# Mixing matrices loaded as f32 on SyncE's queue and cast by ScalarE, with operand tiles by role and chunk stages placed by product slots

## The chip, the cores and the metric

The kernel runs on one core of one Trainium2 chip. The metric is the device time of that core in microseconds (us), the median of several executions. Each execution is sorted as fast or slow; the ratios below use fast ones alone, the medians all. On the profile's pages the engines are PE (TensorE matmuls), PEld (TensorE's weight loads), DVE (VectorE), ACT (ScalarE), POOL (GpSimd) and SP (SyncE). "SPq" and "POOLq" are instructions that an engine only issues, DMAs above all. "L336" is line 336 of that kernel.

## The reference, cut to what matters

```python
# x: 8 x 4224 x 192;  w_tok_r, w_tok_i: 4224 x 4224, all f32
x  = softmax_conv(x, weight)             # 7 taps, 8 groups of channels
theta = x @ w_theta
zr, zi = x * cos(theta), x * sin(theta)
y  = einsum('ts,bsd->btd', w_tok_r, zr) + einsum('ts,bsd->btd', w_tok_i, zi)
u  = x + y
return u + maximum(u @ w_ch, 0)
```

Nearly all the work is in the two 4224 x 4224 mixing matrices. They are read from HBM as f32 and multiplied as bf16.

## The kernel before

The 4224 tokens are 33 chunks of 128. The kernel makes 61 *visits*. A visit takes up to 11 chunks of `zr` and `zi` and (mostly) a pair of 128-row tiles of the output, and forms seven products for each half of a group of columns (a scheme in Strassen's manner, with operands `A11, A21, A22, A12` and their sums `S1` to `S4`). So a visit has 14 *product slots*. With 11 chunks a slot is 11 matmuls of 384 columns, planned at 1.79 us. For such a visit four tiles of weights are loaded, 4 DMAs each, transposed in 32 x 32 blocks by VectorE and summed by VectorE.

Some visits also prepare a chunk for later visits: convolution, two DMA transposes, the `theta` matmuls, clamping, sine and cosine. I call them **chunk visits**. These are visits 15 to 26 and 32 to 43; visits 15 and 32 prepare for the single-tile visits 16 and 33, visits 26 and 43 only finish the last chunk of their group, and the 18 between (17 to 25 and 34 to 42) are the *ordinary* ones. Visits 10 to 14 and 27 to 31 prepare nothing. Visits 0 to 9 are the **start** (1 to 10 chunks each) and 44 to 60 are the **tail**, where results are also finished and stored.

The parts that the change touches:

```python
    wpool = ctx.enter_context(tc.tile_pool(name="wpool", bufs=7))
    spool = ctx.enter_context(tc.tile_pool(name="spool", bufs=4))
    # ... cut
    class Weights:
        # ... cut
        def load(self):
            i = self.loads.pop(0)
            w = moe_w_tok_r if i[2] == "1" else moe_w_tok_i
            t = 2 * self.u + (i[1] == "2")
            st = spool.tile([P, NQ, SLOTS * Q], BF16, name="st", tag="st")
            for a in range(NQ):
                t0 = tokens(self.lo, a)
                nc.gpsimd.dma_start(             # casts f32 to bf16 on the way
                    out=st[a * Q : (a + 1) * Q, :, 0 : self.n * Q],
                    in_=w[t * P : (t + 1) * P, t0 : t0 + self.n * Q].rearrange(
                        "(bt i) s -> i bt s", bt=NQ
                    ),
                )
            self.st[i] = st
    # ... cut: step() transposes st into w by VectorE, or forms a sum S
    def chunk_events(c, t0, n):                  # times in us around t0
        for at, fn in (
            (-15.0, lambda: c + 2 < NCH and load_chunk(c + 2)),
            (-18.0, lambda: (chunks[c].conv(0), chunks[c].conv(1))),
            # ... cut
            (-14.0, lambda: chunks[c].transpose(0)),
            (-13.5, lambda: (chunks[c].transpose(1), chunks[c].keep())),
            (-5.0, lambda: chunks[c].theta(0)),
            (-2.5, lambda: chunks[c].theta(1)),
            (0.0, lambda: chunks[c].wave(0, 0)),
            # ... cut
    for v in range(len(visits)):                 # steps of visit v+1, loads of v+2
        # ... cut
        for frac, fn in (
            (0.4, lambda v=v: (start_weights(v + 2), step(v + 1), loads(v + 2, 1))),
            (2.4, lambda v=v: (step(v + 1), loads(v + 2, 1))),
            (2.9, lambda v=v: (step(v + 1), loads(v + 2, 1))),
            (4.4, lambda v=v: step(v + 1)),
            # ... cut
```

## Time and profile before

| | before |
|---|---|
| median (fastest to slowest) | 1540.75 us, 3 runs (1538.92 to 1586.56) |
| profiled run | 1555.2 us |
| start, up to visit 10 | 208.2 us |
| ten visits without a chunk | 250.2 us, 25.0 each |
| chunk visits | 660.1 us; the ordinary ones 29.0 on average |
| tail | 436.6 us |

A visit is timed from its first product matmul to that of the next, in the trace. These lines are from the page of the kernel before: the span, PE's busy time, then 40 equal slices of the span (the digit is the busy share in tenths; PEclk is the granted clock), and the two DMA queues that carry most of the bytes: queue, packets, MB, share of the 16 engines' time. q0 is GpSimd's queue.

```profile
span 1555.2 us, 25507 instructions
PE 1425.6 (92%) x9390; PEld 869.5 (56%) x9390; DVE 1078.8 (69%) x1818; ACT 336.5 (22%) x582; POOL 743.7 (48%) x1242
PE   5799999999999999999999999989999887878497
DMA  8999966559999999987889999999999999999995
q0 software_dynamic: 178496, 97.84, 49.4%
q1 hardware_dynamic: 94960, 180.56, 38.2%
```

PE is nearly always busy except at the two ends. The table of windows: the first row covers visits 11 to 14, without a chunk; the second covers visits 18 to 25, eight ordinary chunk visits.

```profile
core 0: us, PE busy (x) PEld busy (x) DVE busy (x) ACT busy (x) POOL busy (x), PEclk, DMA share, GB/s
233.30:333.40 100.10, 100.10 (x618) 60.27 (x617) 47.67 (x64) 19.52 (x40) 34.48 (x65) 1.00 0.63 122
403.10:634.70 231.60, 222.74 (x1493) 134.61 (x1490) 173.43 (x289) 47.57 (x81) 87.55 (x160) 0.99 1.10 207
```

Without a chunk PE never stops and DMA stands at a share of 0.63 and 122 GB/s. (The share is summed packet time over the time of 16 engines, and it can pass 1.) In chunk visits DMA is at 1.10 and 207 GB/s, and PE has 231.60 - 222.74 = 8.9 us of holes in eight visits. From the list of waits (engine, line, what it waited for, us in total, times, longest):

```profile
POOL st L327 <- DVE w L347: 429.5, 92, 11.3
PE v L301 <- DMA uT<-xz: 21.0, 15, 4.4
PE y L413 <- DVE d L431: 17.4, 3, 7.1
```

The first of these is harmless: GpSimd waits because its loads are *early* and all four buffers are full. The second is the wait that the new slot placement is aimed at: `theta` waits for the chunk's DMA transpose.

### The profile page before, as it was taken

What the parts mean: (1) busy time and instruction counts of PE and PEld (TensorE: products, weight loads), DVE (VectorE), ACT (ScalarE), POOL (GpSimd) and SP (SyncE); (2) the same over time, 40 slices, a digit from 0 to 9 for tenths busy, and PEclk for the clock granted to TensorE, in tenths of its full rate; (3) what the DMA queues carried; (4) which work ended last, traced back from release to release, by engine and by line L of the source; (5) the groups of instructions that cost most, each with busy time, mean ns of one, the idle gap of its engine ahead of it and who ended that gap; (6) DMA issues with size and microseconds to landing.
All of it is one profiled execution on the core that took longest, in us unless ns stands there. A gap on an engine that the chain in (4) does not pass through costs nothing.

```text
span 1555.2 us, 25507 instructions
## 1 busy us (share of the span) xinstructions
PE 1425.6 (92%) x9390; PEld 869.5 (56%) x9390; DVE 1078.8 (69%) x1818; ACT 336.5 (22%) x582; POOL 743.7 (48%) x1242
## 2 busy tenths in 40 slices
PE   5799999999999999999999999989999887878497
PEld 3455666656556556566665556655665554545354
DVE  6887854437777777776648877867886676667664
ACT  4654322122221221200002212212111111112111
POOL 9775433324334334332324343433577576666451
PEclk8999999999999999999999999999999998989699
DMA  8999966559999999987889999999999999999995
GB/s 103 232 213 194 181 122 126 121 115 207 207 213 203 210 205 205 223 197 177 182 178 203 223 215 205 208 178 208 242 191 218 231 223 201 244 210 224 188 200 133
DMA packets 361580, 301.65 MB, mean 194 GB/s; under 512 B 181008, under 2 KB 307984, under 8 KB 361456
## 3 DMA queue, kind: packets, MB, share of 16 engines
q0 software_dynamic: 178496, 97.84, 49.4%
q1 hardware_dynamic: 94960, 180.56, 38.2%
q10 hardware_dynamic: 88000, 21.64, 11.3%
q8 instruction: 73, 1.20, 0.3%
q14 instruction: 51, 0.42, 0.1%
HBM read 250.21 MB, written 106.56 MB: 229 GB/s over the span
## 4 chain that ended last, share of the span: by engine, by line
PE 61%; DMA 23%; DVE 5%; POOL 4%; issue 3%; ACT 3%; ACTq 1%; SPq 0%; DVEq 0%; POOLq 0%
PE y L413 25%; PE x L413 17%; PE s L413 14%; DMA uT<-xz 10%; PE v L301 3%; DMA ubT<-ubT 3%; DMA uT<-ub 2%; POOL st L327 2%; DMA xr<-xs 2%; DMA st<-in_moe_w_tok_i_dram 2%; PE pc L200 2%; DVE w L347 1%; DMA st<-in_moe_w_tok_r_dram 1%; ACTq L285 1%; DVE w L362 1%
## 5 line engine op out<-in xcount | busy, mean ns | idle before, releaser
L413 PEld LDWEIGHTS <-w 128*128 128x128 bf16 x6600 | 641.7, 98 | 449.2 <-issue 42.0
L327 POOL DMA_DIRECT2D st<-in_moe_w_tok_r_dram x476 | 258.9, 559 | 316.5 <-DVE w L347 194.2
L327 POOL DMA_DIRECT2D st<-in_moe_w_tok_i_dram x476 | 258.4, 558 | 314.2 <-DVE w L347 235.4
L347 DVE STREAM_TRANSPOSE w<-st 128x640 bf16<-128x640 bf16 (+4 forms) x324 | 258.2, 832 | 58.3 <-PE x L413 48.8
L431 DVE TENSOR_TENSOR d<-y,d 128x384 f32<-128x384 f32 x250 | 137.2, 553 | 179.3 <-PE y L413 165.5
L413 PE MATMUL y<-zr,w 128*128 128x384 bf16 x1056 | 191.2, 331 | 22.3 <-DVE d L431 17.4
L413 PE MATMUL x<-zr,w 128*128 128x384 bf16 x1122 | 203.0, 331 | 0.0
L413 PE MATMUL y<-zt,w 128*128 128x384 bf16 x1122 | 199.4, 328 | 3.8 <-ACT y L455 3.8
L413 PE MATMUL x<-zi,w 128*128 128x384 bf16 x1122 | 199.0, 327 | 0.0
L413 PE MATMUL y<-zt,wl 128*128 128x384 bf16 x1056 | 186.2, 330 | 0.0
L413 PE MATMUL s<-zt,w 128*128 128x384 bf16 x1056 | 184.7, 326 | 0.8 <-DVE late L431 0.7
L413 PE MATMUL s<-zi,w 128*128 128x384 bf16 x1056 | 184.7, 328 | 0.0
L362 DVE TENSOR_TENSOR w<-w 128x1408 bf16<-128x1408 bf16 (+10 forms) x174 | 146.8, 843 | 1.7 <-PE s L413 1.4
L413 PEld LDWEIGHTS <-wl 128*128 128x128 bf16 x1056 | 104.1, 99 | 67.7 <-issue 3.3
L243 ACT ACTIVATE zr<-ang,half_pi 128x768 bf16<-128x768 f32 x66 | 59.5, 929 | 318.4 <-PE y L413 238.9
L231 DVE TENSOR_SCALAR ang<-v 128x384 f32<-128x384 f32 x132 | 66.8, 545 | 55.3 <-PE v L301 55.0
L455 ACT ACTIVATE y<-x 128x384 f32<-128x384 f32 x116 | 55.3, 478 | 221.3 <-PE x L413 209.3
L431 DVE TENSOR_TENSOR d<-s,d 128x384 f32<-128x384 f32 x174 | 91.1, 536 | 11.4 <-PE s L413 9.3
L397 POOL TENSOR_TENSOR d<-d,xr 128x768 f32<-128x768 f32 x38 | 62.7, 1654 | 74.1 <-DMA xr<-xs 34.0
L301 PEld LDWEIGHTS <-uT 128*128 128x128 bf16 x704 | 60.9, 100 | 64.0 <-DMA uT<-xz 27.9
L188 POOL DMA_DIRECT2D xw<-in_x_dram x132 | 76.8, 599 | 38.5 <-PE pc L200 34.8
L347 DVE STREAM_TRANSPOSE wl<-st 128x640 bf16<-128x640 bf16 (+5 forms) x104 | 81.2, 814 | 11.7 <-DMA st<-in_moe_w_tok_i_dram 11.7
(72 smaller groups left out, 949.4 us busy)
## 6 DMA issues: line engine op xcount, KB each, us to landing
part<-d SPq DMA_DIRECT2D x172, 384.0 KB, 4.5
d<-part SPq DMA_DIRECT2D x144, 384.0 KB, 4.7
st<-in_moe_w_tok_r_dram POOLq DMA_DIRECT2D x316, 88.0 KB, 5.7
st<-in_moe_w_tok_i_dram POOLq DMA_DIRECT2D x316, 88.0 KB, 4.6
out_dram<-d SPq DMA_DIRECT2D x38, 384.0 KB, 5.8
xs<-xz SPq DMA_DIRECT2D x132, 96.0 KB, 5.3
xr<-xs POOLq DMA_DIRECT2D x66, 192.0 KB, 4.6
xw<-in_x_dram POOLq DMA_DIRECT2D x129, 96.0 KB, 7.9
```

The source lines that it names most:

```text
L188: nc.gpsimd.dma_start(out=self.xw[lo : lo + n, h, :, :], in_=x[:, t0 : t0 + n, :].rearrange("b s d -> s b d"),)
L200: pe(nc.tensor.matmul(pc[half * 2 * Q : (half + 1) * 2 * Q, hh * B * G : (hh + 1) * B * G], lhsT=bands[:, h, :, :].rearrange("p a m -> p ( ...
L231: dve(nc.vector.tensor_scalar(out=af[:, k * 2 * D : (k + 1) * 2 * D], in0=channel_mix(self.xT[g], k, wth), scalar1=-CLAMP, scalar2=CLAMP, ...
L243: act(nc.scalar.activation(out=z[:, g * HN : (g + 1) * HN], in_=self.ang[g], func=AT.Sin, **({"bias": half_pi[:], "scale": 1.0} if i == 0 ...
L301: pe(nc.tensor.matmul(v[:, b * D : (b + 1) * D], lhsT=tT[:, 3 * k + b + i, :], rhs=w[:, 2 * b + i, :], start=(i == 0), stop=(i == 1),), D)
L327: nc.gpsimd.dma_start(out=st[a * Q : (a + 1) * Q, :, 0 : self.n * Q], in_=w[t * P : (t + 1) * P, t0 : t0 + self.n * Q].rearrange("(bt i) s ...
L347: dve(nc.vector.transpose(w[:, c:ce, :, :], st[:, :, c * Q : ce * Q].rearrange("p bt (c j) -> p c bt j", j=Q),))
L362: dve(nc.vector.tensor_tensor(out=flat(o), in0=flat(self.w[p]), in1=flat(self.w[q]), op=op))
L397: nc.gpsimd.tensor_tensor(out=d, in0=d, in1=xr, op=ALU.add)
L413: pe(nc.tensor.matmul(y[:, 0:PC], lhsT=self.w.block(a, c), rhs=zs[c].operand(b, g), start=(start and c == self.lo), stop=(c == self.hi - 1 ...
L431: dve(nc.vector.tensor_tensor(out=o, in0=y[:, 0:PC], in1=o, op=ALU.add))
L455: act(nc.scalar.activation(out=y[g][:, 0:PC], in_=x[g][:, 0:PC], func=AT.Copy))
```

## The change

Its intent is to free GpSimd from writing descriptors for 952 casting DMAs, to place each step of the preparation at a product slot so that it keeps its place however long the visit is, and to keep one operand tile per role. The weights now go as f32 on SyncE's queue into two `raw` buffers. ScalarE casts `raw` into two `st` buffers, and a load may start only when the cast two tiles earlier has been placed. `S3`, `S1`, `S2` and `S4` move into the first slots of their own visit. The core of the diff:

```diff
+    CAST, LOAD = 2.0, 7.0
 ...
-    wpool = ctx.enter_context(tc.tile_pool(name="wpool", bufs=7))
-    spool = ctx.enter_context(tc.tile_pool(name="spool", bufs=4))
+    wpool = ctx.enter_context(tc.tile_pool(name="wpool", bufs=6))
+    spool = ctx.enter_context(tc.tile_pool(name="spool", bufs=2))
 ...
-        t = constp.tile([P, 4, D], BF16, name=name)
+        t = wk.tile([P, 4, D], BF16, name=name, tag="wc", bufs=1)
 ...
-        def load(self):
-            i = self.loads.pop(0)
+        def load(self, i):
             w = moe_w_tok_r if i[2] == "1" else moe_w_tok_i
             t = 2 * self.u + (i[1] == "2")
-            st = spool.tile([P, NQ, SLOTS * Q], BF16, name="st", tag="st")
+            self.raw[i] = raw = spool.tile([P, NQ, SLOTS * Q], F32, name="raw", tag="raw")
             for a in range(NQ):
                 t0 = tokens(self.lo, a)
-                nc.gpsimd.dma_start(
-                    out=st[a * Q : (a + 1) * Q, :, 0 : self.n * Q],
+                nc.sync.dma_start(
+                    out=raw[a * Q : (a + 1) * Q, :, 0 : self.n * Q],
                     in_=w[t * P : (t + 1) * P, t0 : t0 + self.n * Q].rearrange(
                         "(bt i) s -> i bt s", bt=NQ
                     ),
                 )
+
+        def cast(self, i):
+            raw = self.raw.pop(i)
+            st = spool.tile([P, NQ, SLOTS * Q], BF16, name="st", tag="st")
+            cols = slice(0, self.n * Q)
+            act(nc.scalar.activation(out=st[:, :, cols], in_=raw[:, :, cols], func=AT.Copy))
             self.st[i] = st
 
         def tile(self, i):
-            if i == "A22":
-                return wpool.tile([P, SLOTS, NQ, Q], BF16, name="wl", tag="wl", bufs=2)
-            return wpool.tile([P, SLOTS, NQ, Q], BF16, name="w", tag="w")
-
-        def step(self):
-            i = self.todo.pop(0)
+            tag = "S1" if i == "A21" else i
+            return wpool.tile(
+                [P, SLOTS, NQ, Q], BF16, name="w", tag=tag, bufs=2 if i == "A22" else 1
+            )
+
+        def step(self, i):
 ...
+    def chunk_events(c, v):
+        t0, n = starts[v], length(v) / parts(visits[v][0])
+        zr, zi = (10.05, 12.05) if pair(visits[v][0]) else (4.05, 8.05)
         for at, fn in (
-            (-15.0, lambda: c + 2 < NCH and load_chunk(c + 2)),
-            (-18.0, lambda: (chunks[c].conv(0), chunks[c].conv(1))),
-            (-15.0, lambda: (
-                chunks[c].conv(2), chunks[c].conv(3), c == NCH - 1 and last_conv()
-            )),
-            (-14.0, lambda: chunks[c].transpose(0)),
-            (-13.5, lambda: (chunks[c].transpose(1), chunks[c].keep())),
-            (-5.0, lambda: chunks[c].theta(0)),
-            (-2.5, lambda: chunks[c].theta(1)),
-            (0.0, lambda: chunks[c].wave(0, 0)),
-            (0.1, lambda: chunks[c].wave(0, 1)),
-            (1.2, lambda: chunks[c].times_x(0, 0)),
-            (2.0, lambda: (chunks[c].times_x(0, 1), chunks[c].sum(0))),
+            (-4.0, lambda: chunks[c].conv(0)),
+            (-3.5, lambda: chunks[c].conv(1)),
+            (-3.0, lambda: chunks[c].conv(2)),
+            (-2.5, lambda: (chunks[c].conv(3), c == NCH - 1 and last_conv())),
+            (-2.4, lambda: c + 2 < NCH and load_chunk(c + 2)),
+            (-2.0, lambda: chunks[c].transpose(0)),
+            (-1.9, lambda: chunks[c].transpose(1)),
+            (-1.8, lambda: chunks[c].keep()),
+            (zr - 5.0, lambda: chunks[c].theta(0)),
+            (zr - 2.7, lambda: chunks[c].theta(1)),
+            (zr, lambda: chunks[c].wave(0, 0)),
+            (zr + 0.05, lambda: chunks[c].wave(0, 1)),
+            (zr + 0.7, lambda: chunks[c].times_x(0, 0)),
+            (zr + 1.2, lambda: (chunks[c].times_x(0, 1), chunks[c].sum(0))),
+            (zi, lambda: chunks[c].wave(1, 0)),
+            (zi + 0.05, lambda: chunks[c].wave(1, 1)),
+            (zi + 0.7, lambda: chunks[c].times_x(1, 0)),
+            (zi + 1.2, lambda: (chunks[c].times_x(1, 1), chunks[c].sum(1))),
+            (zi + 2.0, lambda: (chunks[c].sum(2), chunks[c].sum(3))),
         ):
-            events.append((t0 + at, fn))
-        for at, fn in (
-            (0.0, lambda: chunks[c].wave(1, 0)),
-            (0.1, lambda: chunks[c].wave(1, 1)),
-            (1.2, lambda: chunks[c].times_x(1, 0)),
-            (2.0, lambda: (chunks[c].times_x(1, 1), chunks[c].sum(1))),
-            (3.6, lambda: (chunks[c].sum(2), chunks[c].sum(3))),
-        ):
-            events.append((t0 + 2 * n * cost + at, fn))
+            events.append((t0 + at * n, fn))
 ...
+    SLOT = {
+        "A11": 2.4, "A21": 4.4, "A22": 6.5, "A12": 8.5,
+        "S3": 14.1, "S1": 14.6, "S2": 15.3, "S4": 17.1,
+    }
+    due = []
     for v in range(len(visits)):
-        t0, n = starts[sequence[v]], length(sequence[v])
+        weights[v] = Weights(v)
         if v == 0:
-            events.append((t0 - 8.0, lambda: (start_weights(1), step(0, 8), loads(1, 4))))
-        for frac, fn in (
-            (0.4, lambda v=v: (start_weights(v + 2), step(v + 1), loads(v + 2, 1))),
-            (2.4, lambda v=v: (step(v + 1), loads(v + 2, 1))),
-            (2.9, lambda v=v: (step(v + 1), loads(v + 2, 1))),
-            (4.4, lambda v=v: step(v + 1)),
-            (4.9, lambda v=v: step(v + 1)),
-            (10.1, lambda v=v: step(v + 1)),
-            (10.6, lambda v=v: (step(v + 1), loads(v + 2, 1))),
-            (11.1, lambda v=v: step(v + 1)),
-        ):
-            events.append((t0 + frac / 14 * n, fn))
+            t0, n = -12.0, 8.0
+        else:
+            t0, n = starts[sequence[v - 1]], length(sequence[v - 1])
+        slot = dict(SLOT)
+        if v and not pair(visits[sequence[v - 1]][0]):
+            slot.update(A11=7.2, A12=14.1)
+        for i in weights[v].todo:
+            t = t0 + slot[i] / 14 * n
+            if v and slot[i] > 14:
+                t = starts[sequence[v]] + (slot[i] / 14 - 1) * length(sequence[v])
+            events.append((t, lambda v=v, i=i: weights[v].step(i)))
+            if i[0] == "A":
+                due.append((t, v, i))
+    due.sort()
+    casts = []
+    for k, (t, v, i) in enumerate(due):
+        at, load = t - CAST, t - CAST - LOAD
+        if k >= 2:
+            at = max(at, due[k - 2][0] + 0.001)
+            load = max(load, casts[k - 2] + 0.001)
+        casts.append(min(at, t - 0.001))
+        load = min(load, casts[k] - 0.0005)
+        events.append((casts[k], lambda v=v, i=i: weights[v].cast(i)))
+        events.append((load, lambda v=v, i=i: weights[v].load(i)))
 ...
-    events.append((200.0, lambda: wch_.append(channel_weights(moe_w_ch, "wch"))))
+    events.append((
+        starts[settled] + 0.5, lambda: wch_.append(channel_weights(moe_w_ch, "wch"))
+    ))
```

More of the change, by code (lines that the diff above doesn't have):

```diff
@@ L311, in __init__ @@
             self.n = self.hi - self.lo
-            self.st, self.w = {}, {}
+            self.st, self.w, self.raw = {}, {}, {}
             if pair(self.u):
-                self.loads = ["A11", "A21", "A22", "A12"]
-                self.todo = ["A11", "A21", "A22", "S3", "S1", "S2", "A12", "S4"]
+                self.todo = ["A11", "A21", "A22", "A12", "S3", "S1", "S2", "S4"]
             else:
-                self.loads = ["A11", "A12"]
                 self.todo = ["A11", "A12"]
-        def load(self):
-            i = self.loads.pop(0)
+        def load(self, i):
             w = moe_w_tok_r if i[2] == "1" else moe_w_tok_i
             t = 2 * self.u + (i[1] == "2")
-            st = spool.tile([P, NQ, SLOTS * Q], BF16, name="st", tag="st")
+            self.raw[i] = raw = spool.tile([P, NQ, SLOTS * Q], F32, name="raw", tag="raw")
             for a in range(NQ):
                 t0 = tokens(self.lo, a)
-                nc.gpsimd.dma_start(
-                    out=st[a * Q : (a + 1) * Q, :, 0 : self.n * Q],
+                nc.sync.dma_start(
+                    out=raw[a * Q : (a + 1) * Q, :, 0 : self.n * Q],
                     in_=w[t * P : (t + 1) * P, t0 : t0 + self.n * Q].rearrange(
@@ L624 @@
     load_chunk(1)
-    weights[0] = Weights(0)
-    for _ in range(4):
-        weights[0].load()
     def idle(n, s):
@@ L652, in last_conv @@
         load_sums()
-    def chunk_events(c, t0, n):
+    def chunk_events(c, v):
+        t0, n = starts[v], length(v) / parts(visits[v][0])
+        zr, zi = (10.05, 12.05) if pair(visits[v][0]) else (4.05, 8.05)
         for at, fn in (
-            (-15.0, lambda: c + 2 < NCH and load_chunk(c + 2)),
-            (-18.0, lambda: (chunks[c].conv(0), chunks[c].conv(1))),
-            (-15.0, lambda: (
-                chunks[c].conv(2), chunks[c].conv(3), c == NCH - 1 and last_conv()
-            )),
-            (-14.0, lambda: chunks[c].transpose(0)),
-            (-13.5, lambda: (chunks[c].transpose(1), chunks[c].keep())),
-            (-5.0, lambda: chunks[c].theta(0)),
-            (-2.5, lambda: chunks[c].theta(1)),
-            (0.0, lambda: chunks[c].wave(0, 0)),
-            (0.1, lambda: chunks[c].wave(0, 1)),
-            (1.2, lambda: chunks[c].times_x(0, 0)),
-            (2.0, lambda: (chunks[c].times_x(0, 1), chunks[c].sum(0))),
-        ):
-            events.append((t0 + at, fn))
-        for at, fn in (
-            (0.0, lambda: chunks[c].wave(1, 0)),
-            (0.1, lambda: chunks[c].wave(1, 1)),
-            (1.2, lambda: chunks[c].times_x(1, 0)),
-            (2.0, lambda: (chunks[c].times_x(1, 1), chunks[c].sum(1))),
-            (3.6, lambda: (chunks[c].sum(2), chunks[c].sum(3))),
-        ):
-            events.append((t0 + 2 * n * cost + at, fn))
@@ L707 @@
         else:
-            v = enter[c] - 1
-            n = visits[v][2] - visits[v][1]
-            assert sequence[v] == v
-            at = 10.05 if pair(visits[v][0]) else 4.05
-            chunk_events(c, starts[v] + at * n * cost, n)
-    def start_weights(v):
-        if v < len(visits):
-            weights[v] = Weights(v)
-    def loads(v, n):
-        if v < len(visits):
-            for _ in range(n):
-                if weights[v].loads:
-                    weights[v].load()
-    def step(v, n=1):
-        if v < len(visits):
-            for _ in range(n):
-                if weights[v].todo:
-                    weights[v].step()
+            assert sequence[enter[c] - 1] == enter[c] - 1
@@ L730 @@
+            chunk_events(c, enter[c] - 1)
+    SLOT = {
[3 more added lines that the diff above has]
+    due = []
     for v in range(len(visits)):
-        t0, n = starts[sequence[v]], length(sequence[v])
+        weights[v] = Weights(v)
         if v == 0:
-            events.append((t0 - 8.0, lambda: (start_weights(1), step(0, 8), loads(1, 4))))
-        for frac, fn in (
-            (0.4, lambda v=v: (start_weights(v + 2), step(v + 1), loads(v + 2, 1))),
-            (2.4, lambda v=v: (step(v + 1), loads(v + 2, 1))),
-            (2.9, lambda v=v: (step(v + 1), loads(v + 2, 1))),
-            (4.4, lambda v=v: step(v + 1)),
-            (4.9, lambda v=v: step(v + 1)),
-            (10.1, lambda v=v: step(v + 1)),
-            (10.6, lambda v=v: (step(v + 1), loads(v + 2, 1))),
-            (11.1, lambda v=v: step(v + 1)),
-        ):
-            events.append((t0 + frac / 14 * n, fn))
+            t0, n = -12.0, 8.0
[11 more added lines that the diff above has]
+                due.append((t, v, i))
```

## The prediction

> **What bounds the kernel now.** TensorE. By the busy table PE is busy 1425.6 of 1555.2 us (92%). In the windows where it streams without a hole (200 to 340 us, 680 to 800 us) PE is busy 40.0 of 40 us and a 384-column matmul takes 162.5 ns; DVE (69%), ACT (22%) and POOL (48%) have slack there. If I charge every matmul columns/2400 us, the trace holds 1362 us of matmul; about 190 us are holes or slowed streaming, in three places:
> - start, 0 to 120 us: 43 us (7 us before the first matmul, then 36). Visits of 1 to 5 chunks take 12 to 17 us each; DVE is busy about 90%.
> - chunk visits, 400 to 1125 us: about 35 us. The list of waits gives 21 us to the theta matmuls (v, L301) waiting for the DMA transpose uT<-xz. It is planned 9 to 11 us ahead; the chain of waits shows 9 to 14 us for it.
> - tail, 1125 to 1555 us: 104 us. Waits for the output transposes (ubT, uT<-ub) 36 us, for late DVE accumulations 22 us, for the output relu-add (L508) 10 us; the chain also passes through POOL weight loads and xr<-xs (15 us once).
>
> **What the change removes.** 952 descriptor-writing DMA issues on POOL, 0.56 us each: 517 us, so POOL falls to about 230 us busy. Little of it is on PE's path: the start (POOL st on the chain from 11 to 18 us) and the tail, where xr queues behind weight loads.
>
> **What it adds.** An f32 load cannot cast on SyncE's queue (the Trainium skill, "DMA: Bandwidth & Descriptors", section "SWDGE vs HWDGE vs iDMA": a cast during DMA needs GpSimd), hence 238 ACT casts. From ACT copies of 384 and 768 columns (478 and 843 ns) I estimate 1.45 us for 1408 columns: about 290 us in all, ACT to about 620 us. SP gets 952 issues of about 0.35 us. 71 MB more are written into SBUF; DMA total about 373 MB. All queues share the same 16 engines (same page, "Issuing engines are not separate DMA queues"), so I expect no bandwidth gain.
>
> **What it moves.** Transposes go seven product slots (12.6 us planned, about 14 real) ahead of theta instead of 9 to 11 us. The S sums move from the preceding visit into the first three slots of their own: less DVE work squeezed into the small visits of the tail, but S1 becomes just-in-time (DVE should finish it about when slot 2 begins). Only two raw buffers: in visits after a small one the third and fourth loads lead their cast by 2 to 5 planned us, below the 4.5 to 6 us landings seen, so ACT and DVE will wait there.
>
> **Sum.** Chunk visits -22 us (the transpose wait nearly gone, S1 costing 0 to 6 back); start -4; tail -13 (fewer late DVE and xr waits, minus cast waits). 1540.75 - 39, rounded: about 1502 us, range 1472 to 1538.
>
> **What would show it.** Right: waits v <- DMA uT<-xz below 5 us; chunk visits 26.5 to 27.5 us instead of 27.5 to 30; POOL near 230 us, ACT near 620; visits without a chunk unchanged at 25.0 us. Wrong: new waits s <- DVE w (S1 late), pc or y <- ACT (ACT stuck behind a cast waiting for its load), a start longer than before.
>
> **What would make it wrong.** f32 loads landing in 9 us or more, blocking ACT in order and with it conv copies, output copies and transposes; SyncE blocked on a store, so that loads slip; the two raw buffers serializing loads at the start (16 issues a visit, two round trips). On the other side the tail could give back 30 us or more, as POOL and small visits are relieved.

## The result, and the profile after

| | before | after |
|---|---|---|
| median (fastest to slowest), 4 runs each | 1539.84 us (1533.15 to 1586.56) | 1732.88 us (1710.82 to 1738.71) |
| ratio of fast runs | | 1.118, 95% interval 1.1036 to 1.1324 |
| start | 208.2 | 225.4 us |
| ten visits without a chunk | 250.2 | 251.7 us |
| chunk visits | 660.1 | 789.0 us |
| tail | 436.6 | 443.0 us |
| profiled run | 1555.2 | 1709.1 us |

A ratio is the mean time of one kernel's fast runs over that of the other's in the same rounds, so it is not quite the ratio of the medians that I quote. Two of the four runs of the changed kernel were slow; the fast ones took 1710.82 (the profiled one) and 1727.24 us. The kernel is 12% **slower**. Of the 154 us between the profiled runs, 129 lie in the chunk visits, 17 in the start and 6 in the tail.

The same lines of the page after:

```profile
span 1709.1 us, 25652 instructions
PE 1484.9 (87%) x9390; PEld 886.1 (52%) x9390; DVE 1077.9 (63%) x1818; ACT 600.3 (35%) x820; POOL 227.9 (13%) x290
PE   4789999998889788899997898888989888778598
DMA  6898966659999999998889999999999999999995
q1 hardware_dynamic: 232048, 323.36, 70.8%
q0 software_dynamic: 41408, 26.41, 10.8%
```

GpSimd is relieved as intended (743.7 to 227.9 us) and ScalarE has taken the casts (336.5 to 600.3 us). The bytes on the two queues rise from 97.84 + 180.56 to 26.41 + 323.36 MB, because SBUF now receives four bytes per weight. PE needs 59 us more for the same 9390 matmuls. The windows of visits 11 to 14 and of visits 18 to 25, columns as above:

```profile
250.50:350.60 100.10, 100.10 (x618) 60.27 (x617) 49.43 (x64) 39.60 (x56) 0.00 (x0) 1.00 0.63 177
436.70:720.10 283.40, 240.48 (x1491) 139.12 (x1489) 174.02 (x289) 90.90 (x113) 18.22 (x32) 0.93 0.97 211
```

Visits without a chunk take as long as before. The eight chunk visits take 283.40 in place of 231.60 us. PE's idle time in them grew from 8.9 to 42.9 us (283.40 - 240.48), and its busy time by 17.7 us. The fall of the clock from 0.99 to 0.93 accounts for that: 0.07 of 283.40 less 0.01 of 231.60 is 17.5 us. Note the DMA columns: the share is *lower* than before and the rate about the same. So this row alone does not prove a full DMA system.

From the list of waits after:

```profile
DVE w L351 <- ACT st L336: 343.1, 138, 11.3
ACT st L336 <- DMA raw<-in_moe_w_tok_r_dram: 295.1, 51, 12.1
ACT st L336 <- DMA raw<-in_moe_w_tok_i_dram: 281.4, 80, 10.8
PE v L302 <- DVE ang L232: 77.2, 20, 7.0
PE v L302 <- DMA uT<-xz: 7.7, 2, 3.9
```

Read them as a chain. The cast waits for the load, the block transpose on VectorE waits for the cast, and the `theta` matmul on PE waits for a clamp (`ang`) that stands behind that transpose on VectorE. Before, loads were waiting for buffers; now everything waits for loads. The transpose wait fell from 21.0 to 7.7 us, so that part worked.

The timeline of visit 21 (540.3 to 574.8 us) shows one such chain. Columns: start, us, engine, line, operation, operands, count, and in brackets the idle time before and its releaser.

```profile
536.55 3.16 ACTq L286 DMA_TRANSPOSE uT<-xz  x2
...
543.37 0.35 SPq L390 DMA_DIRECT2D d<-part  x1
543.81 3.46 SPq L222 DMA_DIRECT2D xs<-xz  x4
...
547.79 1.97 SPq L325 DMA_DIRECT2D raw<-in_moe_w_tok_r_dram  x4
...
555.25 1.38 ACT L336 ACTIVATE st<-raw 128x1408 bf16<-128x1408 f32 x1 [10.68 <-DMA raw<-in_moe_w_tok_r_dram]
...
556.66 1.71 DVE L351 STREAM_TRANSPOSE w<-st 128x640 bf16<-128x640 bf16 x2 [7.27 <-ACT st L336]
...
558.73 1.01 DVE L232 TENSOR_SCALAR ang<-v 128x384 f32<-128x384 f32 x2
559.32 1.44 PE L302 MATMUL v<-wth,uT 128*128 128x192 bf16 x8 [3.93 <-DVE ang L232]
```

Visit 22's load of `A21` is issued at 547.79, where the plan had about 539; SyncE is late because the store and load ahead of it on its queue waited. The records give the cause of part of that: `d<-part` was released by the landing of the first transpose at 543.35, and an `xs` DMA by the second at 546.00, although they use nothing of it. In the compiled program SyncE's and ScalarE's DMAs take the same eight completion semaphores in turn, so a DMA can wait for an unrelated one eight places earlier. The four loads landed between 551.07 and 555.15. Then cast, transpose, clamp and PE follow at once, and PE had stood still for 3.93 us. The windows just after show the second half of the price:

```profile
554.00:557.00 3.00, 1.40 (x9) 0.72 (x8) 0.34 (x1) 1.38 (x1) 0.00 (x0) 1.00 1.06 306
557.00:560.00 3.00, 0.68 (x5) 0.63 (x5) 3.00 (x6) 0.00 (x0) 0.00 (x0) 0.79 1.07 254
560.00:563.00 3.00, 3.00 (x16) 1.77 (x15) 1.28 (x3) 1.38 (x1) 0.00 (x0) 0.65 1.08 236
```

The clock falls to 0.79 and 0.65 around the hole. This is what the Trainium skill, "TensorE: Matmul & The Clock Gate", Part 1, describes: after an idle window of about 3.4 us the array runs at half clock. This trace agrees in direction, with a hole of 3.93 us and a lower clock just after it. The profile's clock is a mean over the window, so values between a half and 1 are to be expected; the trace's own clock record stands at one half from 558.72 to 562.13 us.

### The profile page after: what moved, and what is told of

The parts are those of the page before. It is cut to its first block, busy times and chain, and to the rows that moved or that the text cites. A ratio compares the mean times of both kernels' runs of the same rounds, so it can differ in the third digit from the quotient of the medians.

```text
span 1709.1 us, 25652 instructions
## 1 busy us (share of the span) xinstructions
PE 1484.9 (87%) x9390; PEld 886.1 (52%) x9390; DVE 1077.9 (63%) x1818; ACT 600.3 (35%) x820; POOL 227.9 (13%) x290
## 2 busy tenths in 40 slices
DMA packets 361582, 373.04 MB, mean 218 GB/s; under 512 B 164624, under 2 KB 307984, under 8 KB 361456
## 3 DMA queue, kind: packets, MB, share of 16 engines
q1 hardware_dynamic: 232048, 323.36, 70.8%
q0 software_dynamic: 41408, 26.41, 10.8%
HBM read 250.21 MB, written 106.56 MB: 209 GB/s over the span
## 5 line engine op out<-in xcount | busy, mean ns | idle before, releaser
L417 PEld LDWEIGHTS <-w 128*128 128x128 bf16 x7656 | 752.2, 100 | 575.0 <-issue 97.0
L351 DVE STREAM_TRANSPOSE w<-st 128x640 bf16<-128x640 bf16 (+5 forms) x428 | 343.6, 837 | 369.1 <-ACT st L336 343.1
L336 ACT ACTIVATE st<-raw 128x1408 bf16<-128x1408 f32 (+10 forms) x238 | 280.0, 1177 | 624.4 <-DMA raw<-in_moe_w_tok_r_dram 295.1
L417 PE MATMUL y<-zt,w 128*128 128x384 bf16 x2178 | 393.5, 332 | 35.9 <-ACT y L459 24.9
L417 PE MATMUL s<-zt,w 128*128 128x384 bf16 x1056 | 184.7, 327 | 13.2 <-DVE w L366 13.2
L366 DVE TENSOR_TENSOR w<-w 128x1408 bf16<-128x1408 bf16 (+10 forms) x232 | 183.5, 791 | 3.5
L302 PE MATMUL v<-wth,uT 128*128 128x192 bf16 x528 | 65.6, 274 | 85.8 <-DVE ang L232 77.2
L201 PE MATMUL pc<-xw,bands 96*64 96x192 bf16 x528 | 49.2, 266 | 34.1 <-ACT xz L208 27.9
L208 ACT ACTIVATE xz<-pc 128x384 bf16<-128x384 f32 x132 | 63.2, 488 | 41.1 <-PE pc L201 39.9
L433 ACT ACTIVATE d<-y 128x384 f32<-128x384 f32 x64 | 31.2, 488 | 112.4 <-PE y L417 112.0
L244 ACT ACTIVATE zi<-ang 128x768 bf16<-128x768 f32 x66 | 54.7, 835 | 29.9 <-issue 25.3
```

Source lines behind the costliest of these rows:

```text
L208: act(nc.scalar.activation(out=self.xz[:, :, hp * 2 * G : (hp + 1) * 2 * G].rearrange("p b (h g) -> p h b g", h=2), in_=pc[:, 0 : 2 * B * ...
L244: act(nc.scalar.activation(out=z[:, g * HN : (g + 1) * HN], in_=self.ang[g], func=AT.Sin, **({"bias": half_pi[:], "scale": 1.0} if i == 0 ...
L302: pe(nc.tensor.matmul(v[:, b * D : (b + 1) * D], lhsT=tT[:, 3 * k + b + i, :], rhs=w[:, 2 * b + i, :], start=(i == 0), stop=(i == 1),), D)
L336: act(nc.scalar.activation(out=st[:, :, cols], in_=raw[:, :, cols], func=AT.Copy))
L351: dve(nc.vector.transpose(w[:, c:ce, :, :], st[:, :, c * Q : ce * Q].rearrange("p bt (c j) -> p c bt j", j=Q),))
L366: dve(nc.vector.tensor_tensor(out=flat(o), in0=flat(self.w[p]), in1=flat(self.w[q]), op=op))
```

## The experiments

All 18 kernels gave correct results. The figures for visits, start and tail come from one profiled run each. "Ratio" is to the kernel before, of the same rounds. For e1 to e8 and e18, three to five of the seven runs of the kernel before were slow, so these ratios rest on two to four fast ones. For the large ratios this changes nothing: even the slowest run of the kernel before in any of those rounds took 1581.16 us.

| run | what it is | median us | ratio, 95% interval | ordinary chunk visit, us |
|---|---|---|---|---|
| after | the change | 1732.88 | 1.118 [1.1036, 1.1324] | 34.2 |
| e1_slots_only | before + slot placement of chunk stages | 1544.57 | 1.0045 [0.9934, 1.0156] | 27.9 |
| e2_pool_f32 | after, f32 loads on GpSimd's queue | 1701.55 | 1.1048 [1.0896, 1.12] | 32.5 |
| e3_pe_transpose | after, chunk transposes by PE | 1618.72 | 1.0501 [1.0398, 1.0604] | 29.1 |
| e4_old_stages | after, chunk stages at the old times | 1728.69 | 1.1234 [1.1097, 1.1371] | 35.5 (visits 18 to 25) |
| e5_pool_cast_lead9 | after, casting DMAs, 4 bf16 buffers, no ACT cast | 1555.77 | 1.0101 [1.0019, 1.0184] | 28.4 |
| e6_pool_cast_lead20 | e5, loads 20 us ahead of their step | 1566.77 | 1.016 [1.0073, 1.0248] | 28.4 |
| e7_act_copy_lead20 | e6 + a ScalarE bf16 copy of each tile | 1565.19 | 1.0158 [1.003, 1.0287] | 28.4 |
| e8_spread | after, steps of A21, A22, A12 later | 1710.1 | 1.1107 [1.1022, 1.1192] | 34.0 (visits 18 to 25) |
| e9_bf16_two | e2, load buffers bf16 | 1587.71 | 1.0305 [1.0245, 1.0366] | 28.5 |
| e10_bf16_four | e9, 4 buffers | 1564.26 | 1.0119 [1.0046, 1.0191] | 28.3 |
| e11_best | e5, two placements repaired | 1541.72 | 1.0003 [0.9954, 1.0053] | 27.9 |
| e12_three_control | e9, 3 buffers | 1563.77 | 1.0116 [1.0023, 1.0208] | 28.3 |
| e13_extra_half | e12 + unread DMAs, half of what f32 adds | 1656.87 | 1.0728 [1.0584, 1.0872] | 29.2 |
| e14_extra_full | e12 + unread DMAs, all that f32 adds | 1733.83 | 1.1206 [1.1082, 1.1331] | 31.9 (slow run) |
| e15_extra_half_two | e9 + half, two scratch tiles | 1698.61 | 1.0996 [1.0924, 1.1068] | 30.6 |
| e16_extra_full_two | e9 + all, two scratch tiles | 1768.53 | 1.1437 [1.1379, 1.1495] | 34.9 |
| e17_best_pe | e11, chunk transposes by PE | 1550.96 | 1.0024 [0.9961, 1.0086] | 28.6 |
| e18_extra_ahead | e16, the extra DMA ahead of the loads | 1792.4 | 1.1606 [1.1416, 1.1797] | 35.0 |

### First group: which part of the change?

**The slot placement alone**, put into the kernel before: `chunk_events` as in the changed kernel, loads and tiles as before.

```diff
-            chunk_events(c, starts[v] + at * n * cost, n)
+            chunk_events(c, enter[c] - 1)       # with the new list of slots
```

> The kernel before with one part of the change alone: the chunk stages placed by product slots. Loads stay cast DMAs on GpSimd's queue. If the slots are good in themselves (my prediction said 22 us of gain): waits v <- DMA uT fall from 21 us below 8 us and the time is 1505 to 1530 us. If the slots themselves cause the loss (theta at slot 5 sits close behind the weight transposes on DVE): chunk visits of 31 us or more and a time over 1580 us.

It costs nothing and gains nothing (1.0045, interval across 1). The wait that it was made for did fall, from 21.0 to 7.9 us:

```profile
PE v L301 <- DMA uT<-xz: 7.9, 3, 3.8
```

The ordinary chunk visits became a steady 27.9 us. But visits 15 and 32 rose from 26.1 to about 32 us: for the single-tile visits that follow them, `theta` is placed at slot -0.95 and the transposes at -2, one slot apart, so PE waits there. In the profiled runs the ordinary visits gained 19 us in all and these two gave back 12; start and tail together were 6 us longer. So the slots are not the cause of the loss.

**The queue**: the changed kernel with its f32 loads on GpSimd's queue.

```diff
-                nc.sync.dma_start(
+                nc.gpsimd.dma_start(
                     out=raw[a * Q : (a + 1) * Q, :, 0 : self.n * Q],
```

> The changed kernel with its f32 loads issued from GpSimd's queue instead of SyncE's: same bytes, same casts on ScalarE, same slots. Theory A (SyncE's in-order queue and its turn-taking with the DMA transposes make the loads late): casts wait for raw much less than 577 us, chunk visits 28 to 30 us, time 1540 to 1610 us. Theory B (f32 bytes, or the casts in ScalarE's order, are the loss wherever they are issued): still 1680 us or more.

1.1048 against 1.118: the intervals overlap, so the queue is at most a small part. The loads are now issued on time but land late. Counting from the issue of the first of a tile's four DMAs to the landing of the last, a tile in the ordinary chunk visits took a median of 10.4 us here, and 8.4 in both the kernel before and the changed one. The kernel before issued its loads so early that 8.4 us did no harm. The Trainium skill, "DMA: Bandwidth & Descriptors", section "Issuing engines are not separate DMA queues", says that DMAs of scalar, sync and gpsimd run on the same 16 DMA engines and that another issuer saves only the time of issuing. This pair agrees: POOL fell by 516 us of busy time in the change, and moving the loads back made nothing worse.

**The DMA transposes**: the changed kernel with the chunks' transposes on TensorE.

```diff
-            self.xT.append(transposed(self.xf[:, g * HN : (g + 1) * HN], self.early))
+            self.xT.append(transposed(self.xf[:, g * HN : (g + 1) * HN], True))
```

> The changed kernel with the chunk transposes of the later chunks done by TensorE (as the first 11 chunks do) instead of DMA transposes. Theory A1 (SyncE's DMAs wait for the DMA transposes, 6 to 7 us a chunk visit): waits of SyncE's queue on uT<-xz go to zero, chunk visits shrink from 34.5 to about 30 us, time 1620 to 1660 us although TensorE has about 1 us more work a chunk. Theory B (bytes or casts): time 1700 us or more.

This gave back more than half of the loss (1.0501), although PE has 264 transposes more to do. The f32 loads, the two buffers and the casts are all still there. Chunk visits fell to 29.1 us.

**The old placement of the stages** in the changed kernel:

```diff
-            chunk_events(c, enter[c] - 1)
+            chunk_events(c, starts[v] + at * n * cost, n)   # with the old list in us
```

> The changed kernel with the chunk stages put back at the times of before; loads and tiles as changed. If the new slots are what hurts: chunk visits back to 28 to 30 us, time 1560 to 1610 us. If the loads on SyncE's queue hurt whatever the stages: 1660 us or more, with theta waiting for DVE less (it comes 2 slots later) and SyncE still waiting for uT<-xz.

1.1234: no gain. The placement of the chunk stages neither causes nor cures the loss.

### Second group: f32, buffers, cast step, lead

**Casting DMAs again**, everything else of the change kept:

```diff
-            self.raw[i] = raw = spool.tile([P, NQ, SLOTS * Q], F32, name="raw", tag="raw")
+            self.st[i] = raw = spool.tile([P, NQ, SLOTS * Q], BF16, name="st", tag="st", bufs=4)
 ...
-                nc.sync.dma_start(
+                nc.gpsimd.dma_start(
 ...
         def cast(self, i):
-            # raw -> st by ScalarE (abridged)
+            pass
 ...
-            load = max(load, casts[k - 2] + 0.001)
+        if k >= 4:
+            load = max(load, due[k - 4][0] + 0.001)
```

> The changed kernel's slots, roles and tiles, but weights loaded by casting DMAs on GpSimd's queue straight into four bf16 buffers, issued 9 planned us before the DVE transposes as in the changed kernel; no cast on ScalarE. Theory L (the loads are late because they are issued only 9 us before use, into the burst of transposes and x loads at the visit boundary): still slow, chunk visits 30 us or more, 1590 us or more. Theory C (the f32 bytes and the ScalarE casts are the loss): back to the kernel before, 1520 to 1560 us.

1.0101. So the slots and roles together cost at most about 1 to 2%; the rest of the 12% is in the way the weights are loaded. A longer lead, and then the ScalarE step on top of it:

```diff
-    CAST, LOAD = 2.0, 7.0
+    CAST, LOAD = 2.0, 18.0                      # e6
 ...
         def cast(self, i):
-            pass
+            raw = self.raw.pop(i)               # e7; raw is bf16 here, 4 buffers
+            st = spool.tile([P, NQ, SLOTS * Q], BF16, name="st", tag="st")
+            cols = slice(0, self.n * Q)
+            act(nc.scalar.activation(out=st[:, :, cols], in_=raw[:, :, cols], func=AT.Copy))
+            self.st[i] = st
```

> The same with one number changed: the loads are issued 20 planned us before the DVE transposes (four bf16 buffers allow it, two f32 buffers in the same memory do not). Theory L: DVE no longer waits for loads, chunk visits about 28 us, 1510 to 1550 us, well below e5. Theory C: no difference from e5 beyond 2 per cent.

> As e6, but a ScalarE copy (bf16 to bf16, in the place and number of the casts, two buffers behind it) stands between load and transpose. It puts the ScalarE step back without f32 bytes or late loads. If ScalarE's step is harmless once loads are early: within 2 per cent of e6. If ScalarE's in-order casts are a loss of their own: 1590 us or more.

1.016 and 1.0158. With bf16 loads the lead does not help, and 238 copies on ScalarE cost nothing that can be seen. So the cast's own work is not the cause. Whether a longer lead would help the f32 loads is not tested here: their two buffers don't allow it.

**The steps spread** in the changed kernel, so that `theta`'s clamp no longer stands behind a late transpose:

```diff
-        "A11": 2.4, "A21": 4.4, "A22": 6.5, "A12": 8.5,
+        "A11": 2.4, "A21": 7.5, "A22": 8.4, "A12": 10.4,
```

> The changed kernel with three numbers changed: the weight transposes A21, A22 and A12 stand at product slots 7.5, 8.4 and 10.4 instead of 4.4, 6.5 and 8.5, so that the theta clamps on DVE come before them and their loads come after the burst at the visit boundary. If late loads cost time because theta's clamp waits behind them on DVE: waits v <- DVE ang fall from 77 us below 25 us, 1600 to 1660 us. If the loss is DMA bandwidth or bytes: 1700 us or more.

1.1107. The wait of `v` on `ang` fell from 77.2 to 0.2 us, as intended, but the loss moved: now PE's convolution waits for ScalarE, which is stuck behind casts:

```profile
PE pc L201 <- ACT xz L208: 81.0, 33, 5.8
```

The 77.2 us wait on `ang` was a symptom. Whatever stands behind a late load in order becomes the next wait.

**bf16 buffers in place of f32 ones**, one word of e2. Queue, two buffers, ScalarE step, slots and roles are all unchanged:

```diff
-            self.raw[i] = raw = spool.tile([P, NQ, SLOTS * Q], F32, name="raw", tag="raw")
+            self.raw[i] = raw = spool.tile([P, NQ, SLOTS * Q], BF16, name="raw", tag="raw")
```

> e2_pool_f32 with one word changed: the two load buffers hold bf16 (cast by the DMA) instead of f32. Same queue (GpSimd), same two buffers, same lead, same ScalarE step. Theory N (two loads in flight are too few: each load waits for the cast of the one two before, so one late landing delays all that follow): as slow as e2, 1640 us or more. Theory F (what is slow is the f32 load itself): 1540 to 1580 us as e7.

1.1048 becomes 1.0305. This one word is worth 114 us of median time (1701.55 - 1587.71), most of the loss, though e9 stays a little above the range of theory F. In the profiled runs the chunk visits fall from 759.1 to 672.6 us, the start stays (230.2 and 228.6), the tail falls by 35 us. The tile's landing in the ordinary chunk visits falls from 10.4 to 7.1 us.

**Four buffers in place of two**, bf16 being small enough for it:

```diff
-            self.raw[i] = raw = spool.tile([P, NQ, SLOTS * Q], BF16, name="raw", tag="raw")
+            self.raw[i] = raw = spool.tile([P, NQ, SLOTS * Q], BF16, name="raw", tag="raw", bufs=4)
 ...
-            load = max(load, casts[k - 2] + 0.001)
+        if k >= 4:
+            load = max(load, casts[k - 4] + 0.001)
```

> e9 with four load buffers instead of two, lead still 7 planned us before the ScalarE copy. Theory N: back to 1545 to 1580 us, 5 per cent or more below e9. Theory F: within 2 per cent of e9.

1.0119, and the start falls from 228.6 to 207.1 us. So the two buffers cost about 2 points with bf16 loads, most of it in the start, where a visit is short and its four tiles queue for two places (chunk visits fell by 12.6 us too, but the tail rose by 14.7). Three f32 buffers do not fit: a build of the changed kernel with three stops, as pool `dpool` needs 18 KB per partition and 13.6 are left.

**A version with the best parts** (casting DMAs, four buffers, slots, with convolution and transposes 5 slots earlier ahead of single-tile visits):

```diff
+        pre = 0.0 if pair(visits[v][0]) else 5.0
-            (-4.0, lambda: chunks[c].conv(0)),
+            (-4.0 - pre, lambda: chunks[c].conv(0)),
 ...                                              # and so on to keep()
-        "S3": 14.1, "S1": 14.6, "S2": 15.3, "S4": 17.1,
+        "S3": 10.05, "S1": 10.6, "S2": 15.3, "S4": 17.1,
```

> An attempt at a better version: slots and role tiles kept, weights cast by GpSimd's DMAs into four bf16 buffers (e5), and two repairs: in front of the single-tile visits the conv and transposes come 5 slots earlier (e1 and e5 show about 6 us lost in each of two visits), and S3 and S1 are made at slots 10.05 and 10.6 of the preceding visit (e5 shows 11 us of s <- DVE w). Expected: about 20 us below e5, 1515 to 1540 us, 0 to 2 per cent below the kernel before; if the tail takes the gain back, the same as e5.

1.0003: as fast as before, no faster. Chunk visits are the best of all at 642.7 us, 17 us below the kernel before (whose profiled run was one of its longer ones), but the tail of its profiled run took 444.6 against 436.6 us. Nothing here beats the kernel before.

### Third group: is it the added traffic?

The theory by now ("theory D") was that chunk visits have no DMA throughput to spare: with the DMA transposes in the mix about 6 MB a visit just fit, and f32 makes it 7.4 MB. The rival was that the f32 loads are late for themselves. A control with three bf16 buffers (`bufs=3` in the line of e10, and `k - 3`), and the same with one extra f32 DMA per weight tile into a scratch tile that nobody reads:

```diff
+            extra = spool.tile([P, 704], F32, name="extra", tag="extra", bufs=1)
+            nc.gpsimd.dma_start(
+                out=extra[:, 0:32 * self.n], in_=w[t * P : (t + 1) * P, 0 : 32 * self.n]
+            )
```

(64 in place of 32 for the full amount.)

> Control: bf16 weight loads with the cast in the DMA (GpSimd's queue), three load buffers, ScalarE copy step, slots and roles of the changed kernel. Both theories: near the two- and four-buffer versions, 1560 to 1585 us, ordinary chunk visits about 28.3 us.

> Control plus one f32 DMA per weight tile of half the bytes that the f32 loads add (0.72 MB per chunk visit), into a scratch tile that nobody reads. Theory D (chunk visits have no DMA throughput to spare, so the total traffic sets them): chunk visits about 31 us (6.7 MB at 215 GB/s), time about 1610 to 1650 us. Rival (the f32 loads are late because their two buffers and their cast tie them together, not because of total traffic): chunk visits stay at 28 to 28.7 us and the time within 1% of the control.

> Control plus one unread f32 DMA per weight tile of all the bytes that the f32 loads add (1.44 MB per chunk visit). Theory D: chunk visits 33 to 34.5 us (7.4 MB at 215 to 226 GB/s), time 1660 to 1710 us, at least 1640. Rival: chunk visits 28 to 29 us, time within 2% of the control.

The control was as expected (1.0116). Both extras were far slower, 1.0728 and 1.1206, which the rival had excluded. But not as theory D had it: with half the extra the ordinary chunk visits rose only to 29.2 us (31 expected), with all of it to 31.9 (33 to 34.5 expected), while start and tail lost heavily: the tail took 474.0 and 512.7 us against 422.4. And the runs had a flaw of mine. With one scratch tile each extra DMA must wait for the one before it, and the weight loads stand behind that wait on the same in-order queue. GpSimd sat idle before the extra DMAs for 493 and 541 us in all. So I repeated the pair with two scratch tiles, on the base e9:

```diff
-            extra = spool.tile([P, 704], F32, name="extra", tag="extra", bufs=1)
+            extra = spool.tile([P, 704], F32, name="extra", tag="extra", bufs=2)
```

> The first pair with extra traffic had a flaw: its one scratch tile made each extra DMA wait for the one before it to land (GpSimd idle before it 493 us and 541 us in all), and the weight loads stood behind that wait on the same queue. Here the base is the version with two bf16 load buffers (ratio 1.0305, chunk visits 28.4 us) and the scratch has two tiles, one per load buffer. Half the bytes that f32 adds. Theory D (total traffic): wait of GpSimd before the extra DMAs small (under 100 us), chunk visits 29 to 31 us, ratio 1.05 to 1.08. Rival (the f32 loads themselves are late, traffic of others does not matter): chunk visits 28.4 to 28.8 us, ratio 1.03 to 1.04.

> Same with all the bytes that f32 adds, in as many SBUF bytes as the two f32 buffers took. Theory D: chunk visits 31.5 to 33.5 us, close to the 32.5 us of the version with f32 loads on GpSimd's queue, ratio 1.09 to 1.12. Rival: chunk visits 28.4 to 29 us, ratio below 1.05.

1.0996 and 1.1437: both above what *either* theory gave. Ordinary chunk visits took 30.6 and 34.9 us. But the wait had not gone, 291 and 391 us, and the visits without a chunk rose to 27.8 and 27.7 us on average (278.4 and 276.7 for ten). f32 loads do not do that: in e2 those visits took 25.0 us at a similar amount of traffic. So something besides the bytes written costs time here, probably the wait on the queue. There is a second flaw: the extra DMAs also read more from HBM (321.58 MB with the full amount, e16), which the f32 loads do not (250.21 MB, in the kernel before, the changed one and e2). A last try, with the full amount, put the extra DMA ahead of its tile's loads:

```diff
             self.raw[i] = raw = spool.tile([P, NQ, SLOTS * Q], BF16, name="raw", tag="raw")
+            extra = spool.tile([P, 704], F32, name="extra", tag="extra", bufs=2)
+            nc.gpsimd.dma_start(
+                out=extra[:, 0:64 * self.n], in_=w[t * P : (t + 1) * P, 0 : 64 * self.n]
+            )
             for a in range(NQ):
```

> The extra DMA of the second pair still waited for its scratch tile (GpSimd idle before it 404 us in the full run), and even the visits without a chunk lost 2.7 us each, where f32 loads lose nothing at the same traffic; so that pair overstates. Here the extra DMA (full size, two scratch tiles, two bf16 load buffers) stands ahead of its tile's loads: the one it waits for was issued two tiles earlier and has landed by then. Theory D (traffic): wait of GpSimd before the extra DMAs below 100 us, visits without a chunk 25.0 us, chunk visits 31 to 33 us (f32 loads: 32.5), ratio 1.08 to 1.11. Rival (only the wait on the queue slowed the earlier pairs): chunk visits 28.4 to 29.2 us, ratio 1.03 to 1.05.

1.1606, and the wait was still there:

```profile
POOL extra L324 <- DMA extra<-in_moe_w_tok_r_dram: 196.9, 53, 14.9
POOL extra L324 <- DMA extra<-in_moe_w_tok_i_dram: 186.5, 49, 14.8
```

The reason was again in my experiment. In the trace the extra DMAs go out in bunches of up to eight (two at 460.45 us, say, and one at 475.88, 15 us later): nothing reads them, so I take it that the scheduler was free to place them, and my claim that the one waited for "has landed by then" fell. All five runs agree that more DMA work on the loads' queue makes this schedule much slower. None of them separates traffic from waiting on the queue. **The total traffic is therefore not proven as the cause**, and no wait-free form was found within the runs.

**The other side of the same question** could be tested cleanly: take the transposes out of the DMA where the loads are bf16 (the diff of e3, on e11).

> The repaired slot version without the f32 loads (ratio 1.0003, chunk visits 27.9 us), with the chunks' transposes by TensorE in place of the DMA: can it beat the kernel before? Theory D says that with 6 MB the chunk visits are just at the limit of the DMA, so they should gain at most 1 us each (26.9 to 27.9 us) and pay for 12 transposes of TensorE: ratio 0.98 to 1.0. A rival, that DMA transposes cost chunk visits several us whatever the traffic, would put them at 25.5 to 26.5 us and the ratio below 0.98.

1.0024, chunk visits 28.6 in place of 27.9 us. So in a bf16 version the DMA transposes cost nothing that PE could gain; PE only pays for its own transposes. With e2, e3 and e11 this makes a table of two by two. It is not a clean one: e11 and e17 have four load buffers, no ScalarE step and `S3` and `S1` made earlier, so e9 is the right partner of e2, and bf16 loads with two buffers and PE transposes were not run. The rows below are visits 18 to 25 of, in this order, e11 (bf16, DMA transposes), e17 (bf16, PE transposes), e2 (f32 on GpSimd's queue, DMA transposes), e3 (f32 on SyncE's queue, PE transposes), and then e9 (e2 with bf16):

```profile
400.10:623.40 223.30, 223.30 (x1490) 132.97 (x1489) 175.63 (x289) 48.62 (x81) 89.34 (x165) 1.00 1.12 216
401.90:630.60 228.70, 228.70 (x1587) 138.34 (x1585) 183.11 (x305) 47.31 (x80) 87.05 (x160) 1.00 0.96 197
437.50:697.20 259.70, 233.83 (x1490) 135.94 (x1488) 173.11 (x289) 90.76 (x113) 89.14 (x162) 0.97 1.03 227
429.10:661.70 232.60, 230.22 (x1586) 139.16 (x1585) 180.10 (x304) 88.78 (x112) 18.22 (x32) 1.00 0.95 241
434.50:665.20 230.70, 224.69 (x1490) 132.33 (x1488) 176.22 (x289) 91.56 (x113) 87.55 (x161) 1.00 1.05 209
```

In the first two rows PE is busy in every microsecond (223.30 of 223.30, 228.70 of 228.70): there the chunk visit is bound by PE, at 27.9 us, and DMA keeps up. So 6 MB a visit do fit; with PE as the bound these rows can't say how much more would. In the third row PE has 25.9 us of holes. In the fourth, with the same f32 bytes but no DMA transposes, 2.4 us. And the fourth row has the highest rate of all, 241 GB/s. So 211 GB/s in the changed kernel was no ceiling of the DMA engines as such. The changed kernel itself, with f32 on SyncE's queue and DMA transposes, is the row of 283.40 us shown above, and e3 differs from it in the transposes alone. But the rate is lower while a DMA transpose is in flight. Summed from the packets of visits 18 to 25, the moments in which a chunk's input (`xw<-in_x`) is being loaded have 171 (changed kernel), 181 (e2), 185 (e9), 188 (before) and 201 GB/s (e11), where transposes run at about the same time, against 244 (e3) and 262 GB/s (e17), where there are none. So the transposes do take DMA throughput, in bf16 versions too; there PE doesn't notice it.

In chunk visits f32 loads without DMA transposes are tolerable, DMA transposes with bf16 loads are harmless, and the two together are what the schedule cannot stand.

## Why the prediction was wrong

Point by point:

- TensorE as the bound was right for the visits without a chunk: predicted unchanged at 25.0 us, measured 25.0 in the window of four. For chunk visits it held only as long as the loads were on time.
- The direct costs were right. POOL was predicted near 230 us and is at 227.9. ACT was predicted at 620 and is at 600.3: the 238 casts take 280.0 us where I estimated 290. DMA was predicted at about 373 MB, and the page has 373.04.
- *The transpose wait "nearly gone", below 5 us* was nearly right: 7.7 us, from 21.0. *"Chunk visits -22 us"* was not to be had: in e1, where that wait is gone too, the ordinary chunk visits gained 19 us, but visits 15 and 32 gave back 12, start and tail 6, and the kernel is not faster. In the changed kernel they lost 129 us.
- That `S1` becomes just-in-time was right in kind; 0 to 6 us was too little, as PE's `S1` products waited 13.2 us in all for sums. This, PE waiting for ScalarE (`pc` 27.9 us, `y` 24.9; before 4.6 and 3.8) and a longer start were the three signs that I had listed for "wrong", and all three came. The largest new wait of PE, `v` for `ang` at 77.2 us, was not on the list.
- *"Start -4"* became +17, for which the two buffers are the likeliest reason: in the bf16 version they cost 21.5 us there (e9 to e10). I had named that risk. *"Tail -13"* became +6.
- **The step that failed** is in "What it adds": *"71 MB more are written into SBUF ... so I expect no bandwidth gain"*. The bytes were right, and the sum then charged nothing for them: it took TensorE to be the bound in the chunk visits as well, with the loads hidden behind it. The missing term is the lateness of the f32 loads. It measured 114 us of median time (e2 to e9, where only the type of the load buffer differs), 7.4 points of the 11.8; in the profiled runs 86.5 us lie in the chunk visits and 35 in the tail. In the chunk visits of the changed kernel, taking out the DMA transposes cures most of the loss (e3: 685.4 us in place of 789.0; before 660.1). Of the other points the buffers are about 1.9 (as measured with bf16), the queue 1.3 with overlapping intervals, and what e10 keeps of the change (slots, roles and the ScalarE step) 1.2.
- My list of what could go wrong named the mechanism: *"f32 loads landing in 9 us or more, blocking ACT in order"*. The landings were 10.4 us in e2; in the changed kernel they were 8.4, but the loads could be issued about 9 us late (visit 21), and then the chain cast, block transpose, clamp, PE followed. My range ended at 1538 us and left no room for a loss, although the windows before already showed chunk visits at a DMA share of 1.10 and visits without a chunk at 0.63. I had drawn my judgement of slack from the second kind only.

What is shown: most of the loss needs f32 loads (e9), and in the chunk visits it needs the DMA transposes beside them (e3, e17); it does not come from the cast's work (e7), the placement (e1, e4, e8), or mainly from the queue (e2). Not tested: f32 loads issued earlier into more buffers, which might hide the late landings (the lead was varied with bf16 loads alone, e6). What stays open: *why* the pair is slow. The lower DMA rate beside transposes is measured and fits, but it isn't shown that it is the whole; the order of packets on the shared engines may matter, and ScalarE's queue, where two transposes take 3.16 us to issue in visit 21 and casts stand in order with them (e9 has both and loses little). It also stays open how much of e3's gain comes from the shared semaphores on SyncE's queue. e2 has no weight loads on that queue and is still slow, so they are not the main part.

## What to carry to other kernels

Cost a change of type by the stage that is nearest its limit: look up the DMA share and rate in the windows of that stage, not over the span and not in the stage where the engine has slack. A cast in the DMA that looks like a burden on its issuing engine may be paying for itself by halving the bytes that land; before moving it away, try the one-word version that changes the type alone. When you add traffic to test for contention, first make sure that nothing on the same queue has to wait for it.

## What the Trainium skill lacked or had wrong

- "DMA: Bandwidth & Descriptors", section "Rules for kernel authors", says that a transpose next to ordinary DMAs needs nothing. That is about correct results, and all runs agree. It lacks the cost to the traffic beside it: next to f32 weight loads the DMA transposes made eight chunk visits take 283.40 us in place of 232.60 (changed kernel and e3); next to bf16 loads, no time (223.30 against 228.70 without them), though there too the DMA rate was lower, 201 against 262 GB/s while a chunk's input was loaded (e11 and e17).
- The same page, section "Measured (HBM→SBUF, 128 partitions, SWDGE, issued from GpSimd)", gives 341 GB/s for a 1 MB transfer. No page says what to expect of such a mix. Here f32 loads, partial sums both ways and DMA transposes together gave 211 (changed kernel) and 227 GB/s (e2) over eight visits, and 241 without the transposes (e3).
- The same page, section "SWDGE vs HWDGE vs iDMA", says that a cast during DMA needs GpSimd. It doesn't weigh what giving the cast up costs: f32 in place of bf16 buffers on the same queue took 1701.55 us in place of 1587.71.
- No page that I read tells that DMAs of two issuing engines may share completion semaphores in turn, so that a DMA waits for an unrelated one: in visit 21 SyncE's `d<-part` (issued at 543.37) waited for a transpose of ScalarE's that landed at 543.35.
- "TensorE: Matmul & The Clock Gate", Part 1, was right here: after a hole of 3.93 us the clock in 3 us windows was 0.79 and 0.65, and PE needed 1484.9 us for work that had taken 1425.6.
